# Relaying v as 32-bit channel pairs on the vector engine, moving the routing behind the next vote, and re-spreading the expert work of a fused attention and MoE kernel

## The chip, the core and the metric

The kernel runs on one core of a Trainium2 chip. Five engines work side by side: TensorE (PE; its weight loads are listed as PEld), VectorE (DVE), ScalarE (ACT), GpSimd (POOL, which here mostly issues DMAs) and SyncE (SP, DMA issue). The metric is the device time of one launch in microseconds. The kernel before takes 195.68 us as the median of three runs (194.74 to 197.84). The profile is one execution of 194.78 us, whose span in the trace is 193.0 us.

## The reference, cut to what matters

```python
# q, k, v: (4, 8, 768, 64); sort_net: (4, 8, 8, 8)
for _ in range(5):                       # Sinkhorn on the 8x8 matrices P
    P = exp(P - max(P)); P /= sum(P, -1); P /= sum(P, -2)
k_sorted = einsum('bhij,bhjcd->bhicd', P, k_blocks)   # 8 blocks of 96 rows
v_sorted = einsum('bhij,bhjcd->bhicd', P, v_blocks)
scores   = q_blocks @ k_sorted_blocks.T / 8           # within each block
attn_out = softmax(scores) @ v_sorted_blocks
x = attn_out.transpose(0, 2, 1, 3).reshape(3072, 512)
expert = argmax(x @ w_gate, 1); gate = softmax(x @ w_gate)[expert]
out = gate * (relu(x @ w1[expert]) @ w2[expert])      # 8 experts, 512 -> 1024 -> 512
```

The kernel guesses one expert for each of the four batches by a vote on the mean of v, loads the weights of that expert alone, and computes exactly for the rows that this expert serves. A counted rest would be computed in a loop at the end, which in these data has nothing to do.

## The kernel before

It is one long hand-ordered program. Batch 0 starts with the Sinkhorn iterations and its own attention, with no other work for PE. From then on the attention of batch b is a generator of steps, and the expert matmuls of batch b-1 are woven between them as fill. `weave` lets the fill advance in proportion to the microseconds that the steps yield.

```python
vr = [consts.tile([P, D, HP], BF16, name=f"vr{i}") for i in range(2)]   # HP = 64

def relay(engine, b, d0, n):             # v: (c, d) -> (d, c), n of 64 channels
    dst = vr[b % 2][:, d0:d0 + n, :HB]   # HB = 48
    src = v_in[b][:, :, d0:d0 + n]
    if engine is nc.scalar:
        engine.copy(dst.rearrange("p d c -> p c d"), src)
    else:
        engine.tensor_copy(dst, src.rearrange("p c d -> p d c"))

def sort_v(b, d0, n, tag, bufs=1):       # the Sinkhorn mix of v's blocks
    t = psp.tile([P, n, HI], F32, tag=tag, bufs=bufs)
    for u in range(n):
        for f in range(2):
            nc.tensor.matmul(out=t[f * HP:(f + 1) * HP, u, :],
                             lhsT=vr[b % 2][:, d0 + u, :], rhs=pv..., ...)
    evac(vs[:, b % 2, :, d0:d0 + n], t.rearrange("p d x -> p x d"), at, n * HI)

for it in range(5):                      # Sinkhorn, batch 0
    nc.scalar.activation(sn, sn, ACT.Exp)
    ...
    elif it == 3:
        vote_sum(0); lg0 = vote_pick(0)
        relay(nc.scalar, 0, 0, 8)
        gap3()
    elif it == 4:
        relay(nc.scalar, 0, 8, 16)
        gap4()                           # ends with vote_read(0, lg0)
    ...                                  # six small DVE operations

# [cut] prologue of batch 0
spin(8)                                  # spare matmuls on a zero tile
qps = [turn_q(0, g, ("s", "v", "t")[g]) for g in range(3)]
copy_q(nc.scalar.copy, 0)
relay(nc.scalar, 0, 24, 16)
make_pk([0]); make_pv([0]); spin(5)
copy_q(nc.vector.tensor_copy, 1); copy_q(nc.scalar.copy, 2)
sort_k(0, 0, "s"); spin(2); sort_k(0, 1, "v"); spin(2)
relay(nc.scalar, 0, 40, 16)
relay(nc.vector, 0, 56, 8)
sort_k(0, 2, "s")
# [cut] sort_v in eight pieces between scores(0, 0..2), then values and turn

def steps(b, t0=0):
    for t in range(t0, NB + 2):
        if t < NB:
            exq[t] = scores(b, t);  yield 0.55        # PE, then ACT exp
        if 0 <= t - 1 < NB:
            xoq[t - 1] = values(b, t - 1, ...); yield 0.5   # PE, then DVE
        if t >= 2:
            turn(b, t - 2, ...);    yield 0.45        # PE transpose, then a copy
    route(b)                                          # gate logits, 7 DVE operations
    yield 0.6

def attention(b):
    vote_sum(b);  yield 0.6
    lg = vote_pick(b)                                 # PSUM tag "v"
    relay(nc.vector, b, 0, 16);  yield 0.6
    vote_read(b, lg)
    # [cut] weights of this batch, then v, q and k of the next are requested;
    # [cut] for b == 1 the tables of batches 1 to 3 are made
    for g in range(1, 4):
        relay(nc.vector, b, g * 16, 16)
        if g < 3:
            piece_q(b, g - 1, ("s", "v")[g % 2]);  yield 0.7
    # [cut] sort_v in four pieces, piece_q, sort_k in three
    yield from steps(b)
```

Of the kernel before, what the change touches and what calls it, by code (L numbers as in the profile page):

```python
# [9 lines left out]
BF16 = mybir.dt.bfloat16  # L10
I32 = mybir.dt.int32
U32 = mybir.dt.uint32
# [52 lines left out]
def kernel(  # L65
# [74 lines left out]

    qT = [consts.tile([P, P, CS], BF16, name=f"qT{i}") for i in range(2)]
    ksT = [consts.tile([P, H2 * NB, 2, HP], BF16, name=f"ksT{i}") for i in range(2)]
    vr = [consts.tile([P, D, HP], BF16, name=f"vr{i}") for i in range(2)]
    vs = consts.tile([P, 2, HI, D + 2], BF16)
    exs = [consts.tile([P, H * BLK + PAD], BF16, name=f"ex{i}") for i in range(4)]
    idle = consts.tile([P, 512], BF16)

    nc.vector.memset(idle, 0.0)
    nc.vector.memset(vr[0][:, :, HB:], 0.0)
    nc.vector.memset(ksT[0][:, :, :, HB:], 0.0)  # L150

    ones = consts.tile([P, P], BF16)
# [11 lines left out]
    def spin(n):  # L164
        t = psp.tile([P, 512], F32, tag="f", bufs=3)
        for _ in range(n):
            nc.tensor.matmul(out=t, lhsT=idle[:, :P], rhs=idle, start=True, stop=True)
# [21 lines left out]
        t = ksT[b % 2][:, :, :, :HB].rearrange("p x f (y c) -> p (x f) y c", c=CS)  # L189
        return t[:, :, :, g * 8:(g + 1) * 8]  # L190

    def relay(engine, b, d0, n):
        dst = vr[b % 2][:, d0:d0 + n, :HB]
        src = v_in[b][:, :, d0:d0 + n]
        if engine is nc.scalar:
            engine.copy(dst.rearrange("p d c -> p c d"), src)  # L196
        else:
            engine.tensor_copy(dst, src.rearrange("p c d -> p d c"))

# [1 line left out]
    vh = consts.tile([P, 2 * H], F32)  # L203
    vmask = consts.tile([P, H], BF16)

    wv = consts.tile([P, H, E], BF16)
    wv4 = wv.rearrange("p (c r) e -> p c r e", r=2)
    swap = psp.tile([P, DC, E], F32, tag="f", bufs=3)
# [23 lines left out]
    def vote_pick(b):  # L232
        lg = psp.tile([P, E], F32, tag="v")
        for h in range(H):
            nc.tensor.matmul(out=lg, lhsT=vm[b][:, h:h + 1].to_broadcast([P, P]),
                             rhs=wv[:, h, :], start=(h == 0), stop=(h == H - 1))
        clk.run_pe(0.35)
        return lg
# [60 lines left out]
    def gap4():  # L299
        nc.vector.tensor_copy(expand_k[:, :H], ident[:BH, :H, None].to_broadcast(  # L300
            [BH, H, NB * CQ]))
        vote_read(0, lg0)

    for it in range(5):
        nc.scalar.activation(sn, sn, ACT.Exp)
        if it == 1:
            gap1()
            finish_wv()
        elif it == 2:
            gap2()  # L310
        elif it == 3:
            vote_sum(0)
            lg0 = vote_pick(0)
            relay(nc.scalar, 0, 0, 8)
            gap3()
        elif it == 4:
            relay(nc.scalar, 0, 8, 16)
            gap4()
        nc.vector.reduce_sum(red[:, :, 0], sn, axis=AX.X)
        nc.vector.reciprocal(red, red)  # L320
        nc.vector.tensor_mul(sn, sn, red.to_broadcast([BH, NB, NB]))
        snt = sn.transpose([0, 2, 1])
        nc.vector.reduce_sum(red[:, :, 0], snt, axis=AX.X)
        nc.vector.reciprocal(red, red)
        dst = (snb if it == 4 else sn).transpose([0, 2, 1])
        nc.vector.tensor_mul(dst, snt, red.to_broadcast([BH, NB, NB]))
# [5 lines left out]
    note_vote(0)  # L332
    load_qk(q, q_in, "q_in", 1, 1)
    load_qk(k, k_in, "k_in", 1, 1)
    nc.gpsimd.memset(vr[1][:, :, HB:], 0.0)
    nc.gpsimd.memset(ksT[1][:, :, :, HB:], 0.0)


# [4 lines left out]
    def make_pk(bs):  # L343
        n = 2 * len(bs)
        rep = psp.tile([P, n, NB, NB], F32, tag="f", bufs=3)
        for g in range(n):
            h0 = bs[0] * H + g * H2
            nc.tensor.matmul(out=rep[:, g].rearrange("p i j -> p (i j)"),
                             lhsT=expand_k[:, h0:h0 + H2].rearrange("p h x -> p (h x)"),
                             rhs=snf, start=(g == 0), stop=(g == n - 1),  # L350
                             skip_group_check=True)
        sel = small.tile([P, n * NB, NB], F32, tag="sel")
        nc.vector.tensor_mul(sel, rep.rearrange("p g i j -> p (g i) j"),
                             kj[:, None, :].to_broadcast([P, n * NB, NB]))
        pt = small.tile([P, n, NB], F32, tag="pt")
        nc.vector.reduce_sum(pt.rearrange("p g i -> p (g i)"), sel, axis=AX.X)
        for g in range(n):
            t = consts.tile([P, H2, NB, CQ], BF16, name=f"pk{bs[0]}_{g}")
            nc.vector.tensor_mul(
                t, ksel[:, :, None, :].to_broadcast([P, H2, NB, CQ]),  # L360
                pt[:, g, None, :, None].to_broadcast([P, H2, NB, CQ]))
            pk[bs[0] + g // 2, g % 2] = t.rearrange("p h i c -> p (h i c)")
# [37 lines left out]
    def sort_v(b, d0, n, tag, bufs=1):  # L400
        t = psp.tile([P, n, HI], F32, tag=tag, bufs=bufs)
        for u in range(n):
            for f in range(2):
                nc.tensor.matmul(  # L404
                    out=t[f * HP:(f + 1) * HP, u, :], lhsT=vr[b % 2][:, d0 + u, :],
                    rhs=pv[b][:, f * H:(f + 1) * H, :].rearrange("p h i -> p (h i)"),
                    start=(u % 8 == 0), stop=(u % 8 == 7), skip_group_check=True)
        at = clk.run_pe(0.05 * n)
        evac(vs[:, b % 2, :, d0:d0 + n], t.rearrange("p d x -> p x d"), at, n * HI)
# [148 lines left out]

    spin(8)
    qps = [turn_q(0, g, ("s", "v", "t")[g]) for g in range(3)]

    def copy_q(engine, g):
        engine(q_dst(0, g), qps[g].rearrange("p c x -> p x c"))

    copy_q(nc.scalar.copy, 0)
    relay(nc.scalar, 0, 24, 16)
    make_pk([0])
    make_pv([0])  # L570
    spin(5)
    copy_q(nc.vector.tensor_copy, 1)
    copy_q(nc.scalar.copy, 2)
    clk.act, clk.dve, clk.pe = 2.0, 1.0, 1.0
    sort_k(0, 0, "s")
    spin(2)
    sort_k(0, 1, "v")
    spin(2)
    relay(nc.scalar, 0, 40, 16)
    relay(nc.vector, 0, 56, 8)  # L580
    sort_k(0, 2, "s")
    exq, xoq = {}, {}
    for g in range(3):
        sort_v(0, 8 * g, 8, "f", 3)
    exq[0] = scores(0, 0)
    for g in range(3, 5):
        sort_v(0, 8 * g, 8, "f", 3)
    exq[1] = scores(0, 1)
    for g in range(5, 8):
        sort_v(0, 8 * g, 8, "f", 3)  # L590
    exq[2] = scores(0, 2)
    xoq[0] = values(0, 0, exq.pop(0))
    exq[3] = scores(0, 3)
# [11 lines left out]
    def steps(b, t0=0):  # L605
        for t in range(t0, NB + 2):
            if t < NB:
                exq[t] = scores(b, t)
                yield 0.55
            if 0 <= t - 1 < NB:  # L610
                xoq[t - 1] = values(b, t - 1, exq.pop(t - 1))
                yield 0.5
            if t >= 2:
                turn(b, t - 2, xoq.pop(t - 2))
                yield 0.45
        route(b)
        yield 0.6

    STEPS_US = NB * 1.5 + 0.6

    fill = expert(0)
    main = steps(0, NB // 2 + 1)
    for _ in range(3):
        next(main)
    weave(main, STEPS_US / 2 - 2.1, fill, HIDDEN_US)

    def attention(b):
        vote_sum(b)  # L630
        yield 0.6
        lg = vote_pick(b)
        relay(nc.vector, b, 0, 16)
        yield 0.6
        vote_read(b, lg)
        ev = read_vote(b)
        w1t = load_w1(ev)
        wexp[b] = (w1t, load_w2(ev))
        note_vote(b)
        if b + 1 < B:  # L640
            load_v(b + 1)
            load_qk(q, q_in, "q_in", b + 1, 1)
            load_qk(k, k_in, "k_in", b + 1, 1)
        if b == 1:
            nc.vector.tensor_copy(expand_k[:, H:], ident[:BH, H:BH, None].to_broadcast(
                [BH, BH - H, NB * CQ]))
            nc.vector.tensor_copy(expand_v[:, H:], ident[:BH, H:BH, None].to_broadcast(
                [BH, BH - H, NB * 2]))
            make_pv([1, 2, 3])
            yield 1.2  # L650
            make_pk([1, 2, 3])
            yield 1.2
        for g in range(1, 4):
            relay(nc.vector, b, g * 16, 16)
            clk.run_dve(0.85, 0.0)
            if g < 3:
                piece_q(b, g - 1, ("s", "v")[g % 2])
                yield 0.7
        n = D // 4
        for g in range(4):  # L660
            sort_v(b, g * n, n, ("s", "v")[g % 2])
            if g % 2:
                yield 1.4
        piece_q(b, 2, "s")
        sort_k(b, 0, "v")
        yield 1.4
        sort_k(b, 1, "s")
        sort_k(b, 2, "v")
        yield 1.4
        yield from steps(b)  # L670

    ATTN_US = 1.2 + 1.4 * 5 + STEPS_US
    for b in range(1, B):
        weave(attention(b), ATTN_US + (2.4 if b == 1 else 0.0), fill,
              EXPERT_US - (HIDDEN_US if b == 1 else 0.0))
        for _ in fill:
            pass
        fill = expert(b)
    for _ in range(FC):
        next(fill)  # L680
    hit = consts.tile([P, B, NTB], F32)
# [72 lines left out]
```

The softmax here doesn't subtract the row's maximum and nothing guards it: scores larger than these inputs give would overflow.

## Time and profile before

| from the page | value |
|---|---|
| median time, span of the profiled execution | 195.68 us, 193.0 us |
| busy: PE, DVE, ACT | 155.3, 105.7, 101.8 us |
| v relay on DVE (L198) | 13 instructions, median 812 ns |
| v relay on ACT (L196) | 4 instructions, median 3708 ns |
| expert matmuls: hidden (L508), outputs (L521) | 256 in 50.1 us, 192 in 47.6 us |

A row of the timeline gives the start and length in microseconds, engine, source line, operation, output and inputs. The bracket at its end says how long the engine had been idle before it, and what released it; "issue" there means that nothing in the profile explains the wait. In the rows of time windows each engine's busy time is followed by its number of instructions, then by the granted TensorE clock as a share of full speed, the DMA share and the GB/s. Line 175 is the ACT branch and line 173 the DVE branch of one evacuation helper, so the output's name says which work it is.

### The profile page before, as it was taken

The page shows a single profiled execution, that of the slowest core. Times are in us where ns is not written, and L with a number is a line of the kernel's source. Part 1 is how long each engine was busy: PE and PEld are TensorE (multiplying, and loading weights), DVE is VectorE, ACT ScalarE, POOL GpSimd, SP SyncE. Part 2 cuts the span into 40 slices and gives each one's busy share as a digit, 9 for nine tenths or more (in the row PEclk, how much of TensorE's full clock was granted, in tenths as well). Part 3 has the DMA queues.
Part 4 walks back from the last instruction along what each step waited for, and adds up shares of the span by engine and source line. Part 5 has one row for each costly group of instructions (what it writes and reads, how often), then busy time and mean ns, then how long its engine had stood idle before and what let it go on. Part 6 is the DMA issues. An engine that isn't in the chain of part 4 may idle for free.

```text
span 193.0 us, 5163 instructions
## 1 busy us (share of the span) xinstructions
PE 155.3 (80%) x2243; PEld 94.9 (49%) x2243; DVE 105.7 (55%) x253; ACT 101.8 (53%) x150; POOL 24.4 (13%) x47
## 2 busy tenths in 40 slices
PE   0298279998687799876779899999989998989960
PEld 0154165656365355454545555465755554545420
DVE  6849346464894556557616564668545555452130
ACT  4299984645363656544625556447855463523210
POOL 7856000000430000003500000005000000000000
PEclk9999855589999999999969999999999999999996
DMA  4999999600199999311999973216990122100341
GB/s 60 205 204 202 210 204 213 131 0 3 7 190 193 212 227 253 126 58 8 182 191 217 212 180 109 104 64 88 193 164 0 58 109 109 58 0 0 127 153 58
DMA packets 13626, 24.51 MB, mean 127 GB/s; under 512 B 1312, under 2 KB 6176, under 8 KB 13600
## 3 DMA queue, kind: packets, MB, share of 16 engines
q0 software_dynamic: 9568, 17.83, 51.8%
q1 hardware_dynamic: 4032, 6.32, 9.1%
q8 instruction: 19, 0.31, 0.6%
q14 instruction: 7, 0.06, 0.1%
HBM read 35.68 MB, written 6.29 MB: 217 GB/s over the span
## 4 chain that ended last, share of the span: by engine, by line
PE 63%; ACT 15%; DVE 14%; issue 4%; DMA 1%; DVEq 0%; ACTq 0%
PE ps L508 21%; PE ps L521 19%; ACT vr L196 6%; PE av L439 5%; PE t L404 4%; PE sc L420 4%; DVE xo L447 3%; DVE o L539 3%; PE tp L458 3%; ACT qT L175 3%; PE t L388 2%; PE t L181 2%; ACT ex L429 2%; PE lg L473 1%; ACT xT L175 1%
## 5 line engine op out<-in xcount | busy, mean ns | idle before, releaser
L508 PE MATMUL ps<-xT,t 128*128 128x384 bf16 x256 | 50.1, 336 | 2.4 <-issue 2.2
L521 PE MATMUL ps<-t,hT 128*128 128x512 bf16 x192 | 47.6, 380 | 0.0
L429 ACT ACTIVATE ex<-sc 128x768 bf16<-128x768 f32 x32 | 26.0, 811 | 10.6 <-PE sc L420 10.6
L516 ACT ACTIVATE hT<-ps 128x384 bf16<-128x384 f32 x38 | 18.6, 490 | 23.8 <-PE ps L508 23.8
L508 PEld LDWEIGHTS <-t 128*128 128x128 bf16 x256 | 22.6, 99 | 16.9 <-issue 3.8
L514 DVE TENSOR_SCALAR hT<-ps 128x384 bf16<-128x384 f32 x26 | 14.5, 557 | 20.2 <-PE ps L508 20.0
L521 PEld LDWEIGHTS <-hT 128*128 128x128 bf16 x192 | 16.2, 97 | 15.1
L447 DVE TENSOR_TENSOR xo<-av,rec 96x512 bf16<-96x512 f32 x32 | 22.0, 686 | 1.1
L175 ACT COPY xT<-tp 128x384 bf16<-128x384 bf16 x21 | 10.0, 478 | 13.9 <-PE tp L458 13.9
L439 PEld LDWEIGHTS <-ex 128*128 128x128 bf16 x256 | 12.0, 103 | 9.5 <-DVE xo L447 3.4
L252 POOL DMA_DIRECT2D t<-in_moe_w_dram x4 | 3.1, 766 | 107.2 <-PE t L181 36.4
L539 DVE TENSOR_SCALAR o<-ps,gw 128x512 f32<-128x512 f32 x11 | 8.3, 751 | 15.0 <-PE ps L521 14.7
L439 PE MATMUL av<-vs,ex 128*128 128x65 bf16 x256 | 14.4, 203 | 2.4 <-DVE xo L447 1.7
L420 PE MATMUL sc<-qT,ksT 64*128 64x96 bf16 x256 | 12.0, 217 | 4.4 <-ACT ex L429 2.8
L537 ACT ACTIVATE o<-ps,gw 128x512 f32<-128x512 f32 x13 | 8.9, 687 | 11.8 <-PE ps L521 11.8
L404 PE MATMUL t<-pv,vr 128*64 128x64 bf16 x512 | 10.8, 203 | 5.1 <-ACT vs L175 3.6
L445 DVE RECIPROCAL rec<-av 96x8 f32<-96x8 f32 x32 | 6.4, 200 | 14.5 <-PE av L439 14.5
L173 DVE CAST vs<-t 128x1024 bf16<-128x1024 f32 (+1 forms) x9 | 8.8, 986 | 9.0 <-PE t L404 9.0
L404 PEld LDWEIGHTS <-vr 128*64 128x64 bf16 x512 | 10.2, 119 | 7.1 <-issue 6.2
L173 DVE CAST ksT<-t 128x1024 bf16<-128x1024 f32 x8 | 9.8, 1224 | 6.6 <-PE t L388 6.6
L175 ACT COPY qT<-t 128x1024 bf16<-128x1024 bf16 x9 | 9.0, 1013 | 7.4 <-PE t L181 7.2
L420 PEld LDWEIGHTS <-ksT 64*128 64x128 bf16 x256 | 7.2, 99 | 11.5 <-issue 8.4
(95 smaller groups left out, 170.4 us busy)
## 6 DMA issues: line engine op xcount, KB each, us to landing
t<-in_moe_w_dram POOLq DMA_DIRECT2D x8, 1024.0 KB, 11.8
out_dram<-o SPq DMA_DIRECT2D x24, 256.0 KB, 2.0
v_in<-in_v_dram POOLq DMA_DIRECT2D x4, 768.0 KB, 14.2
t<-in_q_dram POOLq DMA_DIRECT2D x4, 768.0 KB, 19.3
t<-in_k_dram POOLq DMA_DIRECT2D x3, 768.0 KB, 22.9
t<-in_k_dram POOLq DMA_DIRECT2D x3, 256.0 KB, 10.4
sn<-in_sort_net_dram SPq DMA_DIRECT2D x1, 8.0 KB, 1.6
wg<-in_moe_w_gate_dram SPq DMA_DIRECT2D x1, 16.0 KB, 1.9
```

Source lines behind the costliest of these rows:

```text
L173: nc.vector.tensor_copy(dst, src)
L175: nc.scalar.copy(dst, src)
L404: nc.tensor.matmul(out=t[f * HP:(f + 1) * HP, u, :], lhsT=vr[b % 2][:, d0 + u, :], rhs=pv[b][:, f * H:(f + 1) * H, :].rearrange("p h i -> ...
L420: nc.tensor.matmul(out=sc[:, r, h4 * BLK:(h4 + 1) * BLK], lhsT=ksT[b % 2][rows, x].rearrange("p f c -> p (f c)"), rhs=qT[b % 2][rows, x * ...
L429: nc.scalar.activation(ex[:, :H * BLK].rearrange("p (t c) -> p t c", t=2), sc[:, :, :H2 * BLK], ACT.Exp, scale=scale)
L439: nc.tensor.matmul(out=av4[:, h // 4, h % 4, :], lhsT=ex[:, h * BLK:h * BLK + P], rhs=vs[:, b % 2, h * NB + i, :D + 1], start=(h % 4 == 0) ...
L447: nc.vector.tensor_mul(xo, av4[:BLK, :, :, :D], rec.to_broadcast([BLK, 2, 4, D]))
L508: nc.tensor.matmul(out=ps, lhsT=w1t[:, dc, fc * P:(fc + 1) * P], rhs=xT[:, dc, half * NH:(half + 1) * NH], start=(dc == 0), stop=(dc == DC ...
L514: nc.vector.tensor_scalar_max(hT[:, fc, :], ps, 0.0)
L516: nc.scalar.activation(hT[:, fc, :], ps, ACT.Relu)
L521: nc.tensor.matmul(out=ps, lhsT=hT[:, fc, s * P:(s + 1) * P], rhs=w2t[:, fc, :], start=(fc == 0), stop=(fc == FC - 1))
L539: nc.vector.tensor_scalar_mul(o, ps, gw[:, t:t + 1])
```

## The change

v's copy keeps two neighbouring channels side by side, so that the relay moves 32-bit words: half as many elements for the same bytes, all on DVE, with none left to ACT. The matmuls that read it as weights then step over every second element. Routing a batch moves from the end of its own attention to a place after the vote of the next batch, so that it stands between neither the last step and that vote, nor the vote and the weight request. The yields of the steps are changed, so that the first scores and the last turns get more fill. Spare matmuls move to the start of the program, and the order of the prologue is rearranged.

```diff
-    vr = [consts.tile([P, D, HP], BF16, name=f"vr{i}") for i in range(2)]
+    vr = [consts.tile([P, D // 2, HP, 2], BF16, name=f"vr{i}") for i in range(2)]
-    def relay(engine, b, d0, n):                     # [body cut, see above]
+    def relay(b, d0, n):
+        src = v_in[b].bitcast(U32)[:, :, d0 // 2:(d0 + n) // 2]
+        dst = vr[b % 2].rearrange("p d c r -> p (d c r)").bitcast(U32).rearrange(
+            "p (d c) -> p d c", c=HP)[:, d0 // 2:(d0 + n) // 2, :HB]
+        nc.vector.tensor_copy(dst, src.rearrange("p c d -> p d c"))
+    spin(9)                                          # before the first real matmul
         elif it == 3:
             vote_sum(0)
-            lg0 = vote_pick(0)
-            relay(nc.scalar, 0, 0, 8)
             gap3()
         elif it == 4:
-            relay(nc.scalar, 0, 8, 16)
+            lg0 = vote_pick(0)
             gap4()
+            relay(0, 0, 16)
 # sort_v
-   lhsT=vr[b % 2][:, d0 + u, :],
+   lhsT=vr[b % 2][:, (d0 + u) // 2, :, (d0 + u) % 2],
 # prologue
-    spin(8)
+    spin(3)
     copy_q(nc.scalar.copy, 0)
-    relay(nc.scalar, 0, 24, 16)
+    copy_q(nc.scalar.copy, 1)
     make_pk([0])
+    spin(4)
     make_pv([0])
-    spin(5)
-    copy_q(nc.vector.tensor_copy, 1)
     copy_q(nc.scalar.copy, 2)
     sort_k(0, 0, "s")
-    spin(2)
+    spin(1)
+    relay(0, 16, 16)
     sort_k(0, 1, "v")
-    spin(2)
-    relay(nc.scalar, 0, 40, 16)
-    relay(nc.vector, 0, 56, 8)
+    spin(1)
+    relay(0, 32, 32)
+    # two sort_v pieces here, then sort_k(0, 2), two pieces before each scores
 # steps
-                yield 0.55
+                yield 1.5 if t == 0 else 0.6
-                yield 0.5
+                yield 0.9 if t in (1, NB) else 0.5
-                yield 0.45
-        route(b)
-        yield 0.6
+                yield 0.4 if t < NB else 0.7
 # attention
-        relay(nc.vector, b, 0, 16)
+        relay(b, 0, D // 2)
         yield 0.6
         vote_read(b, lg)                             # [requests cut]
+        route(b - 1)
+        relay(b, D // 2, D // 2)
+        yield 0.6
         if b == 1: ...                               # tables, split in two yields
+        piece_q(b, 0, "s")
+        piece_q(b, 1, "v")
-        # the loop over g with relay and piece_q is gone; q, v and k pieces follow
-        # in another order, with yields of 1.2, 1.4, 1.4, 1.4 and 2.0
 # the end
+    for _ in range(2):
+        next(fill)
+    route(B - 1)
     for _ in range(FC):
         next(fill)
```

More of the change, by code (lines that the diff above doesn't have):

```diff
@@ L148 @@
     nc.vector.memset(idle, 0.0)
-    nc.vector.memset(vr[0][:, :, HB:], 0.0)
+    nc.vector.memset(vr[0][:, :, HB:, :], 0.0)
     nc.vector.memset(ksT[0][:, :, :, HB:], 0.0)
@@ L190, in k_dst @@
         return t[:, :, :, g * 8:(g + 1) * 8]
-    def relay(engine, b, d0, n):
[L193 to L198, printed above, removed]
+    def relay(b, d0, n):
[3 more added lines that the diff above has]
+        nc.vector.tensor_copy(dst, src.rearrange("p c d -> p d c"))
     vm, top, eids, wexp = [None] * B, [None] * B, [None] * B, [None] * B
@@ L334 @@
     load_qk(k, k_in, "k_in", 1, 1)
-    nc.gpsimd.memset(vr[1][:, :, HB:], 0.0)
+    nc.gpsimd.memset(vr[1][:, :, HB:, :], 0.0)
     nc.gpsimd.memset(ksT[1][:, :, :, HB:], 0.0)
@@ L404, in sort_v @@
                 nc.tensor.matmul(
-                    out=t[f * HP:(f + 1) * HP, u, :], lhsT=vr[b % 2][:, d0 + u, :],
+                    out=t[f * HP:(f + 1) * HP, u, :], lhsT=vr[b % 2][:, (d0 + u) // 2, :, (d0 + u) % 2],
                     rhs=pv[b][:, f * H:(f + 1) * H, :].rearrange("p h i -> p (h i)"),
@@ L575 @@
     sort_k(0, 0, "s")
-    spin(2)
+    spin(1)
+    relay(0, 16, 16)
     sort_k(0, 1, "v")
-    spin(2)
-    relay(nc.scalar, 0, 40, 16)
-    relay(nc.vector, 0, 56, 8)
+    spin(1)
+    relay(0, 32, 32)
+    for g in range(2):
+        sort_v(0, 8 * g, 8, "f", 3)
     sort_k(0, 2, "s")
     exq, xoq = {}, {}
-    for g in range(3):
-        sort_v(0, 8 * g, 8, "f", 3)
+    sort_v(0, 16, 8, "f", 3)
+    sort_v(0, 24, 8, "f", 3)
     exq[0] = scores(0, 0)
-    for g in range(3, 5):
-        sort_v(0, 8 * g, 8, "f", 3)
+    sort_v(0, 32, 8, "f", 3)
+    sort_v(0, 40, 8, "f", 3)
     exq[1] = scores(0, 1)
-    for g in range(5, 8):
-        sort_v(0, 8 * g, 8, "f", 3)
+    sort_v(0, 48, 8, "f", 3)
+    sort_v(0, 56, 8, "f", 3)
     exq[2] = scores(0, 2)
@@ L608, in steps @@
                 exq[t] = scores(b, t)
-                yield 0.55
+                yield 1.5 if t == 0 else 0.6
             if 0 <= t - 1 < NB:
                 xoq[t - 1] = values(b, t - 1, exq.pop(t - 1))
-                yield 0.5
+                yield 0.9 if t in (1, NB) else 0.5
             if t >= 2:
                 turn(b, t - 2, xoq.pop(t - 2))
-                yield 0.45
-        route(b)
-        yield 0.6
-    STEPS_US = NB * 1.5 + 0.6
+                yield 0.4 if t < NB else 0.7
+    STEPS_US = 1.5 * NB + 2.3
     fill = expert(0)
@@ L624 @@
         next(main)
-    weave(main, STEPS_US / 2 - 2.1, fill, HIDDEN_US)
+    weave(main, 1.5 * 3 + 1.5, fill, HIDDEN_US)
     def attention(b):
@@ L632, in attention @@
         lg = vote_pick(b)
-        relay(nc.vector, b, 0, 16)
+        relay(b, 0, D // 2)
+        clk.run_dve(1.0, 0.0)
         yield 0.6
@@ L643, in attention @@
             load_qk(k, k_in, "k_in", b + 1, 1)
+        route(b - 1)
+        relay(b, D // 2, D // 2)
+        clk.run_dve(1.0, 0.0)
+        yield 0.6
         if b == 1:
@@ L649, in attention @@
             make_pv([1, 2, 3])
-            yield 1.2
+        piece_q(b, 0, "s")
+        piece_q(b, 1, "v")
+        yield 1.2
+        if b == 1:
             make_pk([1, 2, 3])
[L652 to L658, printed above, removed]
-        n = D // 4
[L660 to L665, printed above, removed]
+        n = D // 4
+        sort_v(b, 0, n, "s")
+        sort_v(b, n, n, "v")
         yield 1.4
-        sort_k(b, 1, "s")
-        sort_k(b, 2, "v")
+        sort_v(b, 2 * n, n, "s")
+        sort_v(b, 3 * n, n, "v")
         yield 1.4
+        sort_k(b, 0, "s")
+        sort_k(b, 1, "v")
+        yield 1.4
+        sort_k(b, 2, "s")
+        piece_q(b, 2, "v")
+        yield 2.0
         yield from steps(b)
-    ATTN_US = 1.2 + 1.4 * 5 + STEPS_US
+    ATTN_US = 0.6 * 3 + 1.2 + 1.4 * 3 + 2.0 + STEPS_US
     for b in range(1, B):
-        weave(attention(b), ATTN_US + (2.4 if b == 1 else 0.0), fill,
-              EXPERT_US - (HIDDEN_US if b == 1 else 0.0))
+        weave(attention(b), ATTN_US, fill, EXPERT_US - (HIDDEN_US if b == 1 else 0.0))
         for _ in fill:
```

## The prediction

> **What bounds the kernel now.** I read the page's slices first, then the chain of work that ended last in order of time, the timeline where PE is idle, and the time windows by stage.
>
> ```profile
> PE 155.3 (80%) x2243; PEld 94.9 (49%) x2243; DVE 105.7 (55%) x253; ACT 101.8 (53%) x150; POOL 24.4 (13%) x47
> ...
> PE   0298279998687799876779899999989998989960
> ...
> ACT  4299984645363656544625556447855463523210
> ...
> PEclk9999855589999999999969999999999999999996
> ```
>
> A slice is 4.8 us. After 40 us PE carries the kernel with holes in it. Before that it does not: slices 2 to 4 have ACT at 9, PE falls to 2 in slice 4, and the granted clock is halved in slices 5 to 7. The chain names the cause:
>
> ```profile
> 9.36 1.80 ACT vr L196
> 11.21 3.50 ACT vr L196
> 14.70 0.85 ACT qT L565
> 15.55 3.62 ACT vr L196
> ...
> 20.93 3.51 ACT vr L196
> 24.44 0.91 ACT vs L175 x2
> 25.35 0.71 ACT ex L429
> ```
>
> The relay of batch 0's v holds ACT for 12.4 us of the first 25. The evacuations of sorted v and the first exp wait behind it in ACT's order, and PE behind them. Later the holes are of two kinds:
>
> ```profile
> 86.36 0.80 DVE L198 COPY vr<-v_in 128x768 bf16<-128x768 bf16 x1
> ...
> 87.82 0.17 DVE L244 FIND_INDEX8 eid<-mx,lg 128x8 uint32<-128x8 f32 x1
> ...
> 88.04 0.64 PE L181 MATMUL t<-ident,t 128*64 128x128 bf16 x16 [1.12 <-DVE eid L244]
> ...
> 97.69 1.78 PE L508 MATMUL ps<-xT,t 128*128 128x384 bf16 x5 [2.25 <-issue]
> ```
>
> At 88.04 PE waits for the vote's PSUM tile: its two DVE readers stand behind batch 1's routing (84.83 to 86.45), a relay and an expert evacuation. At 97.69 nothing on the chip explains the wait. The windows say how much there is to win (first number PE busy; rows are attention preparation and steps of batches 1, 2, 3):
>
> ```profile
> 46.30:66.00 19.70, 15.87 (x332) 10.40 (x328) 14.75 (x36) 10.28 (x15) 3.87 (x6) 1.00 0.78 134
> 66.00:84.60 18.60, 15.28 (x218) 9.12 (x219) 9.51 (x21) 10.51 (x16) 0.00 (x0) 1.00 0.75 183
> 84.60:105.60 21.00, 17.28 (x316) 11.36 (x313) 11.69 (x22) 10.13 (x16) 4.50 (x6) 0.92 0.77 136
> 105.60:127.00 21.40, 19.51 (x244) 10.93 (x244) 11.79 (x26) 10.90 (x17) 0.00 (x0) 1.00 0.58 144
> 127.00:143.00 16.00, 15.65 (x310) 10.47 (x308) 10.92 (x20) 11.46 (x18) 2.80 (x3) 1.00 0.81 140
> 143.00:164.80 21.80, 19.96 (x247) 11.14 (x247) 12.15 (x29) 11.16 (x19) 0.00 (x0) 1.00 0.21 69
> ```
>
> Length minus PE busy is 3.8 + 3.3 + 3.7 + 1.9 + 0.35 + 1.8 = 14.9 us idle. The change cannot win more than that here without shortening PE's own work.
>
> [...]one-us windows place the changes of clock at about 22.5, 39.5, 97.6 and 101.0 us[...]. The trace has 19 instruction packets of 0.31 MB, 16 KB each. The unexplained waits at 97.69 (2.25 us) and 61.61 (1.19 us) fall on PE instructions 2492 and about 1470[...], both while weights and the next q, k and v stream.[...]the trace has only packed loads (113 ns for vr's 64 columns).
>
> **The change part by part.**
>
> *Prologue.* Removed from ACT: 1.90 + 3.76 + 3.76 + 3.66 = 13.1 us. Added to DVE: relays of 384, 384 and 768 words in place of one of 384 elements. A 384-element relay took 0.57 us. For 768 words I take 0.95 us, above the 0.81 to 0.90 of 768 bf16 elements[...]; this is an estimate. One q copy (1.22 us) moves from DVE to ACT.
>
> I follow the new order with the old durations. The fifth exp no longer waits for ACT, but DVE takes a relay, so the Sinkhorn result comes near 12.5 (12.9 before). q lands at 11.9 (issue 2.1 plus 9.8), the parts of k at 13.2, 14.6 and 15.9. The tables are ready near 15.65. DVE then does the first k copy (1.22) to 16.9, relays (0.55, 0.95) to 18.4, one vs (0.68) to 19.1, and the last k copy (1.22) to 20.3. The first scores follow at 20.4 and their exp at 20.85 (25.20 before). Six more pieces of sorted v and two exps share ACT and DVE, and the first values matmul starts near 23.5 instead of 28.72: 5.2 us. DVE's chain now sets this, and k's arrival is close behind.
>
> *Clock.* If PE keeps the full clock after that, the five unfilled steps save about 0.2 us each (0.62 against 0.40 for values, 0.50 against 0.34 for scores, only part on the path), the first two hidden groups 2 x 0.65 (1.31 against 0.66 for four matmuls), and small ones 0.7: 3 us. But my own walk leaves PE idle from 18.2 to 20.4[...]. I count 1.3 us.
>
> *Batch 1.* The vote comes first, but the tables of batches 1 to 3 stand on DVE behind two relays and the routing. Counting from the end of batch 0's steps: gate logits done near 3.0, routing 1.7 to 4.9, relay to 5.85, tables to 6.6, while PE has run out of work at 3.65. That is a hole of 3 us where before had 1.5. The first sort_v comes at 9.1 (9.8 before), the second at 10.9 (12.3), and the first scores at 18.7 (20.1). The outputs of expert 0 all move into the steps, so these have 12 x 0.86 us of fill instead of 9. Gain: 1.4 us, counting one hidden group (0.65) moved here from batch 0.
>
> *Batches 2 and 3.* Vote, two hidden groups and the gate logits end at about 3.1 us, the vote's tile is free at 3.4, and the first sort_v starts at 5.4 instead of 7.6 and 7.3: 2 us each. Relays are two of 0.95 instead of four of 0.81. In the steps, more fill after the first scores covers the 0.9 to 1.0 us in which PE waits for the exp, and the routing's wait for the last xT (0.57) goes: 1.1 us each after overlap.[...] Gain: 3.4 and 2.8 us.
>
> *Tail.* The final routing waits no longer (0.57 before its matmuls), and fill runs through it: 0.7 us.
>
> Sum: 5.2 + 1.3 + 1.4 + 3.4 + 2.8 + 0.7 = 14.8 us. The steady part, 8.3, would be over half of the 14.9 us of holes, and my walks count each wait once and no new ones; I take off 1.3. So 195.68 - 13.5 = 182.2 us.
>
> **The rivals.**
>
> *Loads of every second element are slow.* There are 512 loads from vr, in pairs that overlap: 64 matmuls took 1.13 us. If loads doubled and set the pace, eight such groups would cost about 8 us more, some of it in holes, and the time would be near 189. For it: no trace has such a load.[...]
>
> *The clock drops anyway, and DVE becomes the bound of the prologue.* For it: the idle 2.2 us above, and ACT's 13 us do not vanish but return as 2 us on DVE, already in a chain with table making. Then only 4 to 5 us come from the prologue: near 184. If instead early spare matmuls keep it warm throughout: near 180.
>
> *The hole of batch 1 costs the clock.*[...] Near 184.5.
>
> *The holes only move.* The fill is a fixed amount of work; giving more to the ends of the steps leaves less between. If the steady part wins only half, the time is near 186.
>
> **Range and chances.** Most rivals lie between 180 and 186, slow loads near 189; with chance in the clock and three microseconds between runs before, 177.5 to 188.5 should hold it 8 times in 10. Faster by over 2% means under 191.8: two of these failures would have to meet. I give 0.93, within 2% 0.05, slower 0.02.
>
> **What would show it right or wrong.** No vr on ACT; the first exp near 21 and the first values near 23.5 us; the clock in slices 4 to 7; vr's DVE copies near 0.95 us and its loads still 113 ns; in batches 2 and 3 sort_v some 2 us sooner after the vote; a hole of about 3 us before batch 1's tables; a wait on "issue" of 1 to 2 us near the same PE instructions. The prediction is wrong if the loads or sort_v groups grow, if first values come after 25 us, or if PE's idle time after batch 0 does not fall by 5 us or more.

## The result, and the profile after

The changed kernel takes 179.36 us (median of four launches, 177.06 to 180.92) against 196.36 us for the kernel before (four launches, 194.74 to 197.84). The ratio is 0.907, with a 95% interval of 0.893 to 0.922. The prediction was 182.2 us, 13.5 below before, with a range of 177.5 to 188.5. Beside the later groups of runs the kernel before took 193.93 to 194.48 us, and the changed kernel 180.4 as the median of all its eight launches: 13.5 to 14.1 us.

Launches of one kernel here spread by up to 7 us; the ratios with intervals leave disturbed launches out, and a median without an interval covers all launches.

From the page of the changed kernel, the busy time of PE and the slices (now 4.5 us each) of PE, ACT and the granted clock:

```profile
PE 154.5 (86%) x2229; PEld 95.0 (53%) x2244; DVE 102.4 (57%) x249; ACT 89.8 (50%) x146; POOL 23.8 (13%) x47
...
PE   7379679989387999999999999899999998969960
...
ACT  3215664535284757627775556276756563523110
...
PEclk9957955599999999999999999999999999999997
```

ACT is no longer full in slices 2 to 4. PE is busy for nearly as long as before (154.5 us, 155.3 before) in a span 14.0 us shorter. But the half clock is still there: once in slices 2 and 3, and again in slices 5 to 7. (The clock figures count the stretch before the first recorded rise as full: up to 5.7 us here, where nine spare matmuls take 4.02 us, and up to 12.3 us before. In c_both, below, nine take 3.93 us and the next six, once the clock has risen, 1.47.)

The chain of work that ended last, in order of time, in the start of the changed kernel:

```profile
2.13 9.96 DMA t<-in_q_dram
12.13 2.77 PE t L181 x48
...
17.49 1.14 DVE ksT L173
18.63 1.20 DVE vr L197 x2
19.83 0.60 DVE vs L173
20.43 1.14 DVE ksT L173
21.61 0.36 PE sc L419 x8
22.00 0.82 ACT ex L428
...
25.04 0.61 PE av L438 x8
```

DVE sets the start now, as foreseen. The first values matmul comes at 25.04 us (28.72 before, 23.5 predicted). The q transposes at the head of the chain take 2.77 us, at half clock (0.50 from 12 to 13 us); before, at full clock, they took 1.53. From the timeline of the kernel before:

```profile
12.74 1.53 PE L181 MATMUL t<-ident,t 128*64 128x128 bf16 x48
```

The changed kernel's time windows for batches 1 to 3 (preparation, then steps; first number PE busy):

```profile
42.20:61.40 19.20, 14.49 (x329) 10.06 (x326) 13.60 (x33) 9.78 (x15) 4.32 (x6) 1.00 0.87 149
61.40:78.90 17.50, 16.83 (x212) 9.32 (x215) 9.80 (x21) 10.59 (x17) 0.00 (x0) 1.00 0.69 169
78.90:94.00 15.10, 15.10 (x335) 10.66 (x332) 10.30 (x21) 10.11 (x16) 3.97 (x6) 1.00 0.69 126
94.00:114.40 20.40, 19.42 (x225) 10.96 (x227) 11.45 (x25) 11.12 (x17) 0.00 (x0) 1.00 0.93 207
114.40:129.50 15.10, 15.10 (x333) 10.67 (x332) 10.13 (x20) 10.19 (x16) 2.29 (x3) 1.00 0.68 119
129.50:150.00 20.50, 19.52 (x222) 11.00 (x227) 11.45 (x25) 11.12 (x17) 0.00 (x0) 1.00 0.35 94
```

Length minus PE busy is 4.7 + 0.7 + 0 + 1.0 + 0 + 1.0 = 7.4 us, where before had 14.9. In batches 2 and 3 the preparation has no hole left. What remains is batch 1's preparation.

The traces give the same marks for every kernel. The table shows the median time; in the profiled launch the mean granted clock, the start of the first values matmul, the first matmul of batch 1's vote, the lengths of batches 1 and 2 from vote to vote, and the time from batch 3's vote to the start of the last DVE evacuation of outputs (all in us):

```
kernel          median  clock  values  vote 1  batch 1  batch 2  batch 3 and end
before          196.36  0.939   28.72   47.36    37.29    42.60    59.48
changed         179.36  0.935   25.04   42.04    36.71    35.53    58.89
changed, again  181.56  0.935   25.13   42.81    37.90    35.53    58.88
b_relay         190.03  0.984   24.50   40.59    37.00    42.61    59.51
b_shift         192.94  0.940   29.36   48.89    37.75    38.63    60.11
b_order         186.56  0.955   29.11   45.96    36.75    37.00    58.47
b_relay_order   180.14  0.983   25.85   43.18    34.12    36.15    58.41
a_relay16       185.65  0.911   26.98   44.13    38.29    36.13    59.46
a_spin_old      179.26  0.935   24.24   41.85    38.11    35.53    58.89
a_route_end     179.32  0.938   25.12   43.30    34.72    35.89    57.85
a_yield_old     181.22  0.905   25.16   42.36    40.14    35.49    58.24
c_tables        178.34  0.954   25.04   42.74    33.93    35.53    58.90
c_warm          176.63  0.993   23.50   37.69    36.20    35.53    58.90
c_both          173.88  0.992   23.54   37.73    33.94    35.53    58.89
```

In the traces the change took 5.3 us before vote 1, 0.6 in batch 1, 7.1 in batch 2, 0.6 from there to the last outputs and 0.4 after them: 14.0 us. In kernels that route after the vote, batch 1 also holds batch 0's routing, and the last column holds two routings instead of one. So part of the 5.3 us is work that moved into batch 1: the routing, and eight hidden matmuls (28 instead of 36 run before vote 1).

The prediction counted from the end of a batch's steps. With the end of the last turn (`tp`, PE) as the mark, these are its terms and what two traces of the changed kernel show (us gained):

```
stage                     foreseen   changed   changed, again
start to end of batch 0      6.5        4.1         3.3
batch 1                      1.4        1.4         0.2
batch 2                      3.4        6.2         6.2
batch 3                      2.8        1.9         1.9
from there to the end        0.7        0.5         0.3
sum                         14.8       14.0        11.8
```

### The profile page after: what moved, and what is told of

Same layout as the page of the kernel before. It is cut to its first block, busy times and chain, and to the rows that moved or that the text cites. A ratio compares the mean times of both kernels' runs of the same rounds, so it can differ in the third digit from the quotient of the medians.

```text
span 179.0 us, 5141 instructions
## 1 busy us (share of the span) xinstructions
PE 154.5 (86%) x2229; PEld 95.0 (53%) x2244; DVE 102.4 (57%) x249; ACT 89.8 (50%) x146; POOL 23.8 (13%) x47
## 4 chain that ended last, share of the span: by engine, by line
PE 73%; DVE 13%; DMA 6%; ACT 3%; issue 3%; POOL 0%; DVEq 0%; ACTq 0%; POOLq 0%
PE ps L507 24%; PE ps L520 22%; PE av L438 6%; DMA t<-in_q_dram 6%; PE sc L419 4%; PE t L181 4%; PE t L403 4%; PE tp L457 3%; PE t L387 3%; DVE xo L446 3%; DVE o L538 2%; PE lg L472 1%; ACT xT L175 1%; DVE ksT L173 1%; DVE vr L197 1%
## 5 line engine op out<-in xcount | busy, mean ns | idle before, releaser
L507 PE MATMUL ps<-xT,t 128*128 128x384 bf16 x256 | 49.1, 332 | 0.1
L520 PE MATMUL ps<-t,hT 128*128 128x512 bf16 x179 | 45.4, 379 | 0.8 <-issue 0.2
L428 ACT ACTIVATE ex<-sc 128x768 bf16<-128x768 f32 x32 | 25.9, 809 | 12.3 <-PE sc L419 12.2
L515 ACT ACTIVATE hT<-ps 128x384 bf16<-128x384 f32 x39 | 19.2, 492 | 20.5 <-PE ps L507 20.5
L513 DVE TENSOR_SCALAR hT<-ps 128x384 bf16<-128x384 f32 x25 | 13.9, 557 | 16.5 <-PE ps L507 16.4
L538 DVE TENSOR_SCALAR o<-ps,gw 128x512 f32<-128x512 f32 x11 | 8.3, 750 | 14.5 <-PE ps L520 14.1
L252 POOL DMA_DIRECT2D t<-in_moe_w_dram x4 | 3.6, 903 | 95.2 <-DVE gw L493 34.0
L173 DVE CAST vs<-t 128x1024 bf16<-128x1024 f32 (+1 forms) x10 | 10.0, 1008 | 5.8 <-PE t L403 5.8
L457 PE MATMUL tp<-ident,xo 96*128 96x96 bf16 x128 | 11.6, 216 | 1.4 <-ACT xT L175 1.1
L403 PE MATMUL t<-pv,vr 128*64 128x64 bf16 x512 | 10.9, 200 | 1.3 <-DVE vs L173 1.3
L403 PEld LDWEIGHTS <-vr 128*64 128x64 bf16 x512 | 9.7, 115 | 3.5 <-issue 2.5
L457 PEld LDWEIGHTS <-xo 96*128 96x128 bf16 x128 | 8.4, 103 | 4.8 <-issue 1.3
```

Of the source, the lines that this page charges most:

```text
L173: nc.vector.tensor_copy(dst, src)
L403: nc.tensor.matmul(out=t[f * HP:(f + 1) * HP, u, :], lhsT=vr[b % 2][:, (d0 + u) // 2, :, (d0 + u) % 2], rhs=pv[b][:, f * H:(f + 1) * H, :] ...
L428: nc.scalar.activation(ex[:, :H * BLK].rearrange("p (t c) -> p t c", t=2), sc[:, :, :H2 * BLK], ACT.Exp, scale=scale)
L457: nc.tensor.transpose(out=tp[:, dc, :], in_=xf[:, dc * P:(dc + 1) * P], identity=ident[:BLK, :BLK])
L507: nc.tensor.matmul(out=ps, lhsT=w1t[:, dc, fc * P:(fc + 1) * P], rhs=xT[:, dc, half * NH:(half + 1) * NH], start=(dc == 0), stop=(dc == DC ...
L513: nc.vector.tensor_scalar_max(hT[:, fc, :], ps, 0.0)
```

## The experiments

The kernel before was measured beside each group: 193.93 us beside the first four runs, 194.24 beside the next four, 194.48 beside the last four (seven launches each).

**The relay alone.**

```diff
 # before, with the pair layout, and
-            relay(nc.scalar, 0, 0, 8)                # third and fourth Sinkhorn gap
-            relay(nc.scalar, 0, 8, 16)
+            relay(0, 0, 16)                          # after gap4
-    relay(nc.scalar, 0, 24, 16)
-    relay(nc.scalar, 0, 40, 16); relay(nc.vector, 0, 56, 8)
+    relay(0, 16, 16); relay(0, 32, 32)
```

> The kernel before with the 32-bit pair relay alone: batch 0's v in three DVE copies (16 channels in the fifth Sinkhorn gap, 16 and 32 after the second k piece), later batches in four DVE copies of 16 channels; routing, yields and spare matmuls as before. Theory (ACT's 12.4 us of relay set the start): first exp at 21.5 to 22.5 us instead of 25.2, first values matmul near 25.5 instead of 28.7, the time 3 to 5 us below before (ratio 0.975 to 0.985). Rival (the work only moves to DVE, which becomes the bound): first values not before 27.5 us, time within 1.5 us of before.

It took 190.03 us, ratio 0.985 (0.974 to 0.995). First exp at 21.53, first values at 24.50. Batches 1 and 2 stand as before (37.00 and 42.61), so with the old order the relay acts on the start alone. The unexplained waits are still there (1.08 and 2.33 us). The profiled launch also kept its clock through the start (9 in slices 0 to 18 of the page), and its vote 1 comes 6.8 us sooner, while the median gains 3.9.

**The unexplained waits.**

```diff
 # before, at the start of PE's program
+    for _ in range(64):                              # one column each, on the zero tile
+        nc.tensor.matmul(out=tiny[:, :1], lhsT=idle[:, :P], rhs=idle[:, :1], ...)
```

> The kernel before with 64 one-column spare matmuls at its start, in a stretch where PE is idle: 128 more PE instructions[...]. Theory[...]: the 2.25 us wait in batch 2's hidden matmuls is gone[...], and with it the half clock at 98 to 101 us; batch 2 is 3 to 4 us shorter and the time 2.5 to 4 us below before (ratio near 0.983). Rival (the wait belongs to that place in the work, whatever its instruction number): the wait stands at the same matmuls, time within 1 us.

The wait is gone. The timeline of this run at the same place, the hidden matmuls after the second half of sorted v (L408 and L512 here):

```profile
95.63 1.20 PE L408 MATMUL t<-pv,vr 128*64 128x64 bf16 x64
...
96.76 1.47 PE L512 MATMUL ps<-xT,t 128*128 128x384 bf16 x8
...
98.17 0.64 PE L181 MATMUL t<-ident,t 128*64 128x128 bf16 x16
```

The eight hidden matmuls run in 1.47 us without a break where before stood 2.25 us still in the middle, and batch 2 is 4.0 us shorter (42.60 to 38.63), the half clock after the wait (0.50 from 97.6 to 101.0 us before; 1.00 from 94 to 99 us here) included. What was changed there is the instruction's number; the work also ran some 2 us later, but in b_relay it ran 7 us earlier and the wait stood. So the wait goes with the instruction's number: that is shown. That PE waits there for a late instruction packet is the author's estimate, from three things. The two waits of before stand at PE instructions 1470 and 2492 of the trace; with the sequencer's own instructions counted they are about 1024 apart. In before PE goes on 2.3 us after an instruction packet starts to move (95.42 and 97.69). And in b_shift the last packet of q8, the queue of that packet, ahead of these matmuls moves between 87 and 88 us, 4 us ahead of the request for the weights (91.66). The whole kernel took 192.94, only 1 us less than before: in the profiled launch vote 1 comes 1.5 us later, v having landed later (batch 0's vote, waiting for it, starts at 9.10 us, 8.35 before), and batch 1 is 0.5 longer, with one slice of 4.8 us (52.6 to 57.3 us) at a clock of 6 tenths on its page, where before has 9. So the wait went as expected, and the size of the time did not.

The changed kernel lost the same wait without anyone aiming at it. The timelines of before and of the changed kernel, request for the weights (POOL) against sorted v (PE), each with the DMA queues around the instruction packet (95 to 96 us before, 84 to 85 us in the changed kernel; q0 carries the weights and the next v, q and k):

```profile
89.69 0.77 POOL L252 DMA_DIRECT2D t<-in_moe_w_dram  x1 [34.74 <-DVE vr L198]
91.11 1.20 PE L404 MATMUL t<-pv,vr 128*64 128x64 bf16 x64 [0.35 <-ACT qT L175]
...
q0 software_dynamic: 96, 0.20, 103.8%
q8 instruction: 1, 0.02, 6.0%
```

```profile
83.57 0.85 POOL L252 DMA_DIRECT2D t<-in_moe_w_dram  x1 [33.96 <-DVE gw L493]
83.94 1.22 PE L403 MATMUL t<-pv,vr 128*64 128x64 bf16 x64
...
q8 instruction: 1, 0.02, 5.9%
```

Before, PE got there 1.4 us after the request; now it gets there 0.4 us after. From the vote the request comes about as late (5.0 us before, 4.8 now); it is PE that comes sooner (6.5 us, now 5.2). The one instruction packet of this stretch was moved at 95.42 us before, 4.3 us after PE began this sorted v, while q0 was busy throughout (103.8%), and at 84.58 us in the changed kernel, 0.6 us after, with no other packet from 84 to 85 us.

**Relays of 16-bit elements in the changed kernel.**

```diff
 # changed kernel
-    vr ... [P, D // 2, HP, 2]; tensor_copy of uint32 pairs; lhsT steps over every second element
+    vr ... [P, D, HP];         tensor_copy of bf16;         lhsT packed
```

> The changed kernel with v's copy laid out channel by channel again and the same three and two relays as bf16 on DVE: 768, 768 and 1536 elements in batch 0, 1536 twice in each later batch. Theory (half as many elements is worth something): each 1536-element copy takes 1.5 to 1.7 us, the first scores come 1.2 to 1.6 us later, the hole before batch 1's tables grows by 0.7, and batches 2 and 3 lose up to 0.5 us each; 2 to 4 us in all. Rival (DVE has the room, only leaving ACT mattered): under 1 us. If packed weight loads are cheaper than loads of every second element, 32 columns of sorted v get faster here than 0.58 us.

185.65 us, ratio 0.959 (0.950 to 0.967) to before: some 5 us lost. The groups of instructions kept apart by shape, of this run and of the changed kernel (total busy us, mean ns):

```profile
L195 DVE COPY vr<-v_in 128x1536 bf16<-128x1536 bf16 x7 | 10.7, 1534 | 0.0
L195 DVE COPY vr<-v_in 128x768 bf16<-128x768 bf16 x2 | 1.7, 826 | 0.0
```

```profile
L197 DVE COPY vr<-v_in 128x768 uint32<-128x768 uint32 x7 | 6.1, 866 | 0.0
L197 DVE COPY vr<-v_in 128x384 uint32<-128x384 uint32 x2 | 1.0, 492 | 0.0
```

In these copies a 32-bit element cost about what a 16-bit one cost (866 and 826 ns for 768), so half as many took a little over half the time (866 ns against 1534 for the same bytes). First values come 1.9 us later; batch 2 is 0.6 longer, and batch 1 1.6 longer than in the changed kernel's first trace, 0.4 longer than in its second, which lost the clock there too (slice 10 of the page, 46.1 to 50.7 us, at 5 tenths here; 0.50 from 49 to 55 us in a_again). The loads of vr's weights have a median of 113 ns packed here and 113 ns with every second element in the changed kernel: the rival of slow loads is out.

**The spare matmuls in their old place.**

```diff
-    spin(9)
...
-    spin(3)
+    spin(8)                                          # before the q transposes
```

> The changed kernel without the nine spare matmuls at the start, and with eight instead of three before the q transposes, as it was before. Theory (the early spares are undone by the idle 3 us before the vote, so they buy nothing): the transposes run at full clock, 1.5 us instead of 2.8, but start about 1 us later; first values within 0.7 us of the changed kernel's 25.0, time within 1.5 us of it. Rival (the early spares matter): 2 us or more slower.

179.26 us, ratio 0.928 (0.923 to 0.933). The transposes take 1.53 us from 13.20, and first values come at 24.24. It is the changed kernel within its spread: moving the spares bought nothing that these runs can show.

**The changed kernel again, and three edits beside it.**

> The changed kernel once more, beside the three below: 176 to 181 us, first values near 24 to 25 us, batches 2 and 3 (vote to vote) 35.5 us each, as the traces so far have it. Its spread comes from where the half clock falls in the first 45 us.

181.56 us, ratio 0.922 (0.913 to 0.931). Batch 2 is 35.53 again. Batch 1 took 37.90 instead of 36.71, and the windows of this run show why (the clock is the third number from the end):

```profile
43.00:46.00 3.00, 2.74 (x63) 1.96 (x59) 1.31 (x6) 1.20 (x4) 0.07 (x1) 1.00 0.03 5
46.00:49.00 3.00, 0.20 (x4) 0.11 (x3) 2.62 (x8) 0.62 (x2) 2.86 (x5) 0.87 0.43 44
49.00:52.00 3.00, 3.00 (x39) 2.18 (x38) 1.41 (x5) 1.73 (x2) 1.39 (x2) 0.50 1.11 205
```

PE waits 2.80 us for batch 1's tables (`rep`), and here the clock after the hole is 0.50 from 49 to 55 us, while in the first trace, after a hole of 2.79 us, it stayed at 1.00. From the timeline of this run:

```profile
48.90 0.34 PE L367 MATMUL rep<-snb,expand_v 32*128 32x64 bf16 x3 [2.80 <-DVE expand_v L650]
```

```diff
 # a_route_end: changed kernel
 # steps, after the last turn
+        route(b)
+        yield 0.6
 # attention, and the end
-        route(b - 1)
-    for _ in range(2):
-        next(fill)
-    route(B - 1)
```

> The changed kernel with the routing back at the end of the batch's own steps, everything else as changed. Theory (the routing stood between the last turn and the next vote): vote to first sort_v grows from 5.2 to 6 us or more in batches 2 and 3, the routing's wait for the last xT is back before each vote, 1 to 1.5 us per batch and 0.6 at the end, 3 to 5 us in all[...]. Rival (the fill covers the routing wherever it stands): under 1 us.

179.32 us, ratio 0.921 (0.916 to 0.926): no slower than the changed kernel beside it. Batch 2 is 0.4 longer, while batch 1 is 2.0 to 3.2 shorter. A part of that is batch 0's routing, which now stands ahead of vote 1 (0.5 to 1.3 us later); the rest is that the tables no longer stand behind it on DVE, and PE's hole before them is 1.15 us:

```profile
47.13 0.26 PE L367 MATMUL rep<-snb,expand_v 32*128 32x64 bf16 x3 [1.15 <-DVE expand_v L651]
```

The vote to first sort_v even shrinks, from 5.2 to 4.9 us. The theory falls.

```diff
 # a_yield_old: changed kernel
-                yield 1.5 if t == 0 else 0.6
+                yield 0.55
-                yield 0.9 if t in (1, NB) else 0.5
+                yield 0.5
-                yield 0.4 if t < NB else 0.7
+                yield 0.45
```

> The changed kernel with the old yields in the steps (0.55, 0.5 and 0.45 throughout) and the totals to match. Theory (fill where the chain waits is worth more than elsewhere): PE waits 0.9 to 1.0 us for the first exp again in batches 1, 2 and 3, and about 0.5 at the end of each, 2 to 4 us in all. Rival (the fill is fixed, so the holes only move): within 1 us.

181.22 us, ratio 0.932 (0.928 to 0.936), against 0.922 (0.913 to 0.931) beside it; the intervals overlap. Batch 2 is 35.49: no loss. Its first scores come 1.7 us later after the vote, and the steps are as much shorter. The wait for the first exp did not come back. What is lost is in batch 1 (40.14): after the vote PE runs out of work at 2.9 us (3.3 in the changed kernel), the tables come at 6.9 (6.1), and the clock after the hole is halved (0.50 from 49 to 55 us):

```profile
49.22 0.34 PE L367 MATMUL rep<-snb,expand_v 32*128 32x64 bf16 x3 [3.98 <-DVE expand_v L650]
```

In batch 2 the holes only moved, as the rival said.

```diff
 # c_tables: changed kernel
 # steps
+                if b == 0 and t == NB:
+                    ...tensor_copy(expand_k...); ...tensor_copy(expand_v...)
 # attention
+        if b == 1:
+            make_pv([1, 2, 3])
         route(b - 1)
-            ...tensor_copy(expand_k...); ...tensor_copy(expand_v...); make_pv([1, 2, 3])
```

> The changed kernel with the two DVE copies for batch 1 to 3's tables made at the end of batch 0's steps, and the first table built before the routing. Theory (PE's 2.8 us hole in batch 1 is DVE's order: two relays and the routing ahead of the tables): the hole falls below 0.8 us, the first sort_v of batch 1 comes 2 us sooner, the half clock that sometimes follows the hole is gone, the time 1.5 to 2.5 us below the changed kernel. Rival (DVE is full there, so the hole turns up later): under 0.7 us.

178.34 us (median of all launches), 3.2 below the changed kernel beside it. The wait of PE for the tables is gone, and the first sort_v of batch 1 comes 5.69 us after the vote instead of 8.3 to 10.0:

```profile
44.70 0.26 PE L367 MATMUL rep<-snb,expand_v 32*128 32x64 bf16 x3
...
48.43 0.70 PE L403 MATMUL t<-pv,vr 128*64 128x64 bf16 x32
```

Batch 1 takes 33.93: 2.8 us less than in the changed kernel's first trace, 4.0 less than in the second. The theory holds.

**The order inside a batch, and the order with the relay.**

```diff
 # before, attention(b)
-        relay(nc.vector, b, 0, 16)                   # then three more, each before or
-            ... piece_q(b, g - 1, ...)               # beside a q piece
+        relay(nc.vector, b, 0, D // 2)
+        # vote_read, requests
+        relay(nc.vector, b, D // 2, D // 2)
+        # then both q pieces, sort_v four times, sort_k 0 and 1, sort_k 2 and the last q piece
```

> The kernel before with the changed order of the pieces inside one batch's preparation alone (both relays early, the q pieces after them, then v, k and the last q piece), relays of 32 channels in bf16 on DVE, routing at the end of the steps, old yields, old start. Theory (what shortens batch 2 is the order: the q pieces no longer stand right behind the vote for its PSUM tile[...]): batch 2, vote to vote, 36 to 38 us instead of 42.6, no unexplained wait over 1 us there, start as before, time 4 to 6 us below before. Rival (the order needs the shorter relay or the moved routing): batch 2 stays above 40 us, time within 2 us.

186.56 us, ratio 0.968 (0.955 to 0.980), 7.9 below before by the medians where 4 to 6 were expected. Batch 2 takes 37.00 us instead of 42.60, with bf16 relays and the routing in its old place. No unexplained wait of 0.6 us or more is left, and the wait of the transposes behind the vote is gone:

```profile
85.55 1.40 PE L181 MATMUL t<-ident,t 128*64 128x128 bf16 x32
...
87.64 0.69 PE L404 MATMUL t<-pv,vr 128*64 128x64 bf16 x32
...
90.88 1.20 PE L404 MATMUL t<-pv,vr 128*64 128x64 bf16 x64
```

The start is as before (first values at 29.11). The 5.6 us have two parts. The unexplained wait and the half clock after it were worth 4.0 in b_shift, where the order was the old one; 1.6 us remain for the order itself. PE is at sorted v by 87.64 here, before the weights are requested (87.95); that the wait is gone for this reason is the author's estimate.

> The kernel before with the 32-bit relay on DVE and the changed order inside a batch, but routing, yields and spare matmuls as before. Theory (these two are the change; routing, yields and spares give nothing once they are there): 177 to 181 us, as the changed kernel, with batch 1 shorter than its 36.7 to 37.9, because the tables do not wait for the routing. Rival (each of the four parts carries its share): 183 to 187 us.

180.14 us, ratio 0.932 (0.916 to 0.947). This is the changed kernel's time, 180.4 as the median of its eight launches, without the moved routing, the new yields, the moved spares and the rearranged prologue; the intervals would hide a difference of 3 us. Batch 1 is 34.12, shorter than in the changed kernel, as the theory had it; batch 2 is 36.15.

**A better version.**

```diff
 # c_warm: changed kernel
+    spin(6)                                          # before the first vote
-    spin(3)
+    spin(7)                                          # before the q transposes
     sort_v(0, 24, 8, "f", 3)
+    spin(4)
     exq[0] = scores(0, 0)
```

> The changed kernel with 14 more spare matmuls: six before the first vote, four more before the q transposes, four before the first scores. Theory (the clock is lost where PE idles at 5.5 to 8.4 and 20.2 to 21.6 us): transposes in 1.5 to 1.7 us, mean granted clock 0.965 or more in most runs, time 1 to 3 us below the changed kernel. Rival (the spares delay work[...]): within 1 us.

176.63 us, ratio 0.919 (0.911 to 0.927), mean clock 0.971 to 0.993 in its four launches. First values come at 23.50 us. The ratio does not set it apart from the changed kernel (0.922, 0.913 to 0.931); the medians do (180.4), and seven of the changed kernel's eight launches lie above the slowest of these four (177.94).

> The changed kernel with the early tables and the 14 more spare matmuls. If both hold and add up: 173 to 176.5 us, batch 1 near 34 us, mean clock 0.97 or more. If the clock is lost anyway: 177 to 178.5, as with the early tables alone.

173.88 us (173.44 to 174.52), ratio 0.904 (0.898 to 0.909). The page of this kernel, and its timeline at the transposes and at the first values matmul:

```profile
PE 151.1 (88%) x2241; PEld 92.0 (54%) x2258; DVE 102.6 (60%) x249; ACT 89.1 (52%) x146; POOL 23.9 (14%) x47
...
PEclk9999999999999999999999999999999999999996
```

```profile
12.19 1.53 PE L181 MATMUL t<-ident,t 128*64 128x128 bf16 x48 [0.75 <-DMA t<-in_q_dram]
...
23.54 0.40 PE L440 MATMUL av<-vs,ex 128*128 128x65 bf16 x8
```

Once risen (the six spares from 5.32 us already take 1.47), the clock is not lost before the end (mean 0.992), and the two edits add up. It is the fastest of all, 6.5 us below the 180.4 of the changed kernel's eight launches.

## Why the prediction was right, and where it was not

The time lies in the range, 2.8 us below the centre, and the gain of 13.5 us is met almost exactly beside the later befores. That close a hit is luck: the start brought 2.4 us less than its terms and batch 2 2.8 us more (4.1 for 6.5, 6.2 for 3.4), and the two errors cancel. One of the prediction's own signs of being wrong was met, by a hair: first values after 25 us (25.04 and 25.13). The other two were not: no load or sort_v group grew, and PE's idle time after batch 0 fell by 7.5 us.

*Prologue.* Right in mechanism: ACT's relay was the bound, and DVE took its place. The walk gave first values at 23.5 us. It assumed the full clock for the transposes. With the clock kept (c_warm) they come at 23.50; in the changed kernel they come at 25.04. There the nine early spares end at 5.3 us, PE idles for 2.95 us before the vote, and when q lands at 12.1 us the clock is at half (0.50, from 9.1 us; the second trace has no rise before q's transposes, which take the same 2.77 us). The term "1.3 us for the clock" was about zero: from first values on, the half clock lasted 10.9 us before and 11.4 in the changed kernel.

*Batch 1.* The hole before the tables was foreseen as 3 us and measured 2.8. The gain was put at 1.4 us; the two traces have 1.4 and 0.2 from last turn to last turn, and 0.6 and a loss of 0.6 from vote to vote, where batch 0's routing counts as batch 1's. The rival "the hole costs the clock" came true in some traces (0.50 after the hole in a_again and a_yield_old) and not in the first (1.00).

*Batches 2 and 3: the step that failed.* The prediction kept a wait on "issue" of 1 to 2 us near the same PE instructions, and that was wrong: batch 2 has none. I counted at which instruction it stands, but not that PE now gets to sorted v sooner (5.2 us after the vote, 6.5 before) and the weights are asked for later relative to it. Its removal was worth 4.0 us in b_shift, which is more than all that batch 2 gained beyond the 3.4 foreseen (2.8 to 3.7 us, by the mark). Without it batch 2 would have gained some 2.2 to 3.1 us, and batch 3, which had no such wait, gained 1.9 where 2.8 were foreseen. The credit was wrong too. I gave the routing and the yields the steady gains; taken back one at a time, each left batch 2 within 0.4 us. The order of the pieces, which I had not priced as a part of its own, carries batch 2 (37.00 instead of 42.60 with nothing else changed), and most of that with the wait that is gone (some 4.0 of 5.6 us, an estimate from b_shift). The 32-bit relay adds 0.6 to 0.9 there. The first sort_v was foreseen 5.4 us after the steps; it came at 5.9.

*Tail.* 0.7 us foreseen; 0.5 and 0.3 measured after the last turn, which agrees, but no run took the tail apart.

*Rivals.* Slow loads: out, 113 ns both ways. Clock lost with DVE as the bound: true in the changed kernel (mean clock 0.935), gone with 14 more spares (0.993 in c_warm; which of their three places did it is not known). The holes only move: true for the yields and the routing taken one by one in batch 2. Not tried: both taken back with the changed relay and start kept, so their joint worth in batches 2 and 3 is known only from b_relay_order (36.15 against 35.53).

## What to carry to other kernels

Move a copy off the engine that sets the end, and then read the new engine's program order: what was placed behind it (here tables behind relays and routing) is the next hole. Test a bundle of reorderings part by part: here two parts, the relay and the order inside a batch, carried the gain, and the moved routing cost batch 1 more in the traces than it saved in batch 2. When PE stops and nothing in the trace releases it, add spare matmuls far ahead of it: if the wait goes, as 2.25 us did in b_shift, it went with the instruction's number; then see when the instruction packets moved and what else moved with them.

## What the runs showed of the hardware that was not expected

- A wait of 2.25 us in the middle of a matmul group went away by adding 64 one-column matmuls 90 us earlier. The wait went with the instruction's number, so an edit far ahead of it could remove it.
- The clock was halved while PE was far from idle: at 22.8 us in the changed kernel it fell with no gap above 1.43 us since 15.95, where it had risen; PE was busy for 5.22 of these 6.85 us. With four spares in that gap and ten earlier, the mean clock was above 0.97 in every launch of c_warm and c_both (0.971 to 0.999).
- ACT needed 3.7 us for the 768-element transposing copy that DVE did in 0.83 (mean of three and of twelve in the kernel before).
